# A new issue order for a fused block-sparse attention and SwiGLU kernel: batch 1's V loads before the second half of the output weights, seven more pairs of zero matmuls

## The chip, the cores and the metric

The kernel runs on one core of one Trainium2 chip. TensorE (PE) multiplies matrices and writes to eight banks of PSUM, VectorE (DVE) and ScalarE (ACT) read PSUM and work element by element, GpSimd (POOL) and SyncE (SP) mostly start DMA transfers. Each engine works through its own queue in program order and waits where an instruction needs something that is not there. The metric is the device time of one execution in microseconds, the median of several runs.

## The reference, cut to what matters

```
# attention: B, H, S, D = 4, 8, 768, 64; blocks of 32
scores = scale * np.matmul(q, k.transpose(0, 1, 3, 2))
mask = (|blk_i - blk_j| <= 1) | first or last block in i or j | 3 sampled key blocks per query block
attn = exp(where(mask, scores, -1e9) - max);  attn = attn / (sum(attn) + 1e-9)
attn_out = np.matmul(attn, v)
x = attn_out.transpose(0, 2, 1, 3).reshape(3072, 512)
# feed-forward: d_model 512, d_ff 1536
xn = x / sqrt(mean(x * x) + 1e-6) * rms_g
g = xn @ w_gate;  silu = g * (1 / (1 + exp(-g)))
out = (silu * (xn @ w_val)) @ w_out          # float32, 3072 x 512
```

Inputs and output are float32; the kernel computes its products in bf16.

## The kernel before

The 3072 rows are cut into 12 chunks of 256 queries (`ch` or `u`, 0 to 11), three for each of the 4 batches. The work is cut into some 1,500 named tasks, each with a function that emits its instructions on one engine. For a chunk and a pair of heads `pr` (0 to 3):

- `s<n>` (L648): scores of two key blocks of 128 for a pair of heads, with n = 12 ch + 3 pr + j2, into two PSUM banks; 4 matmuls over 64 rows of the array, two of which run side by side. Chunk 0 adds its mask by matmuls (L653), the others by a multiplication.
- `x<ch>_<pr>_<j2>_<e>` (L661): the exp on ScalarE, one for each bank. `m<ch>_<pr>_<j2>` (L668): the mask product on VectorE.
- `av<ch>_<pr>` (L678): 24 matmuls of probabilities with V (and a column of ones for the sums). `on` (L690, L692): division by the sums on VectorE.
- `sq`, `rs`, `sc` (L703 or L706, L711, L717): RMS norm, the power on GpSimd. `xd` (L741): transposes of x by DMA from SP; chunks 0 and 1 use TensorE (`xt`) and a copy (`xc`).
- `g<u>_<f>a`, `g<u>_<f>` (L835): two times 16 matmuls of gate and value, side by side over 64 rows each; then `th` on ScalarE (L842), `uu` and `h` on VectorE (L846, L853); f is 0 to 5.
- `y<u>_<t>_<part>` (L868): the product with `w_out` in six parts of two matmuls; parts 0 to 2 read the first half of `w_out` (`wo0_`), parts 3 to 5 the second (`wo1_`). `yo` (L890) copies to SBUF and stores from SP.

Loads: batch 0 comes in by small transfers at the start. For batches 1 to 3, K, Q and V (`l<b>_1_*`, `l<b>_0_*`, `l<b>_2_*`, two halves each, L275) go one after the other from GpSimd's queue into one float32 buffer, `stage`: Q cannot start before K's casts have read it (`c<b>_1_*`), nor V before Q's casts (`c<b>_0_*`), nor the next batch's K before V's casts (`va<b>_*`). All casts are L269 and go to ScalarE or VectorE. `dt<b>_*` (L519) then transposes K and Q by DMA from SP. GpSimd also loads the gate and value weights (`wg0_` to `wv2_`, L452) and `wo0_`, `wo1_` (L458). `w<i>` (L321) is a pair of matmuls on zeros that nobody reads; 14 more of them stand at the very start.

The order in which all this is emitted, and so the order in each engine's queue, is written out in the string `ORDER`. A word is a task, `*ENGINE` picks the engine, and the digits after the colon are the buffers that it takes (PSUM banks 0 to 7 first). `ORDER` came out of a planner, whose costs still stand in the calls of `plan.add`, but the class in the file only reads names, engines, functions, dependencies and pools:

```
def add(self, name, engines, fn, deps=(), acq=(), **_):
    self.tasks[name] = (list(engines), fn, [d.lstrip(">") for d in deps],
                        [p for p in acq if p in self.slots])
```

`run` goes through `ORDER` word by word. It asserts that all tasks named in `deps` come earlier and calls the function.

The words of the order before around the second half of `w_out`:

```
... m2_3_2 l1_2_0 wo1_ one1
l1_2_4 s38:47 s39:15 ... va1_0*DVE va1_1*DVE va1_2*DVE va1_3*DVE s41:47 g1_3a:15
... y0_0_0:4 y0_0_1 s44:72 s45:03 y0_0_2 y0_0_3 y0_0_4 y0_0_5 av3_0:6
```

Of the kernel before, what the change touches and what calls it, by code (L numbers as in the profile page):

```python
# [15 lines left out]
sta0 bm q48 rr cast1_0*DVE tsq0 cast0_0*ACT k45 kind0 t0_1_0:0 t0_0_0:1 kr0:2 bs tsq1 e0_1_0*ACT kc0*ACT  # L16
e0_0_0*ACT cast1_1*ACT kind1 w0:3 mq0:4 kr1:5 mq1:6 mq2:7 t0_1_2:0 mqc0*DVE kc1*ACT mqc1*ACT mqc2*ACT
e0_1_2*ACT cast1_2 cast1_3 cast0_1 s0:32 t1_1_0:1 t1_0_0:4 s1:56 s2:70 x0_0_0_0:0 x0_0_0_1 e1_1_0*DVE
e1_0_0*DVE x0_0_1_0 x0_0_1_1 t2_1_0:3 t2_0_0:2 s3:14 s4:56 k67 V0 V4 gB one0 qrest wg0_ wv0_ wg1_ wv1_ wg2_
wv2_ e2_0_0*DVE e2_1_0*DVE x0_0_2_0 x0_0_2_1 x0_1_0_0:1 x0_1_0_1 x0_1_1_0 x0_1_1_1 s5:27 mt1_2:0 mt2_1:3  # L20
t3_1_0:1 t3_0_0:4 w1:5 s6:65 x0_1_2_0 x0_1_2_1 mk2_1*DVE e3_0_0*DVE mk1_2*DVE va0_0*DVE e3_1_0*DVE x0_2_0_0:2
x0_2_0_1 s7:34 mt1_1:2 s8:07 mt0_2:6 s9:51 mk1_1*DVE x0_2_1_0 mk0_2*DVE x0_2_1_1 x0_2_2_0 x0_2_2_1 x0_3_0_0:3
x0_3_0_1 va0_2*DVE av0_0:3 s10:24 s11:60 av0_2:7 t0_0_2:5 mt2_0:1 va0_1*DVE on0_0 on0_2 e0_0_2*DVE va0_3*DVE
mk2_0*DVE x0_3_1_0 x0_3_1_1 x0_3_2_0 x0_3_2_1 sta1_1 t1_0_2:3 mt1_0:2 s12:47 av0_3:6 s13:50 e1_0_2*ACT
x1_0_0_0:4 x1_0_0_1 x1_0_1_0 mk1_0*DVE m1_0_0 on0_3 x1_0_1_1 s14:31 av0_1:4 s15:27 s16:50 t2_0_2:6 x1_0_2_0
x1_0_2_1 on0_1 sq0_0*DVE sq0_1*DVE x1_1_0_0:0 e2_0_2*DVE x1_1_0_1 x1_1_1_0 x1_1_1_1 l1_1_0 l1_1_4 wo0_ rs0
t3_0_2:3 s17:41 w2:2 w3:2 w4:7 w5:2 s18:76 s19:25 mt0_1:0 x1_1_2_0 x1_1_2_1 mk0_1*ACT x1_2_0_0:2 x1_2_0_1
x1_2_1_0 m1_0_1 sc0_0:0 sc0_1:1 e3_0_2*DVE w6:4 w7:4 xt0_0:10 xt0_1:4 s20:07 s21:36 x1_2_1_1 x1_2_2_0 x1_2_2_1
x1_3_0_0:3 xc0_0*DVE xc0_1*DVE m1_1_1 m1_1_2 m1_0_2 m1_2_1 m1_1_0 qk0 raw0 rawq1 xc0 w8:1 w9:2 g0_0a:12 g0_0
s22:45 s23:07 x1_3_0_1 th0_0:0 x1_3_1_0 x1_3_1_1 x1_3_2_0 x1_3_2_1 uu0_0:0 m1_2_2 h0_0:0 m1_3_0 m1_2_0  # L30
g0_1a:36 g0_1 s24:41 g0_2a:50 s25:72 g0_2 th0_1:1 x2_0_0_0:1 x2_0_0_1 x2_0_1_0 x2_0_1_1 th0_2:2 uu0_1:1 h0_1
m1_3_2 uu0_2:2 av1_0:4 s26:17 mt2_2:3 av1_2:2 s27:65 on1_0 m1_3_1 c1_1_0*DVE mk2_2*ACT x2_0_2_0 x2_0_2_1
x2_1_0_0:4 x2_1_0_1 c1_1_1*DVE c1_1_2*DVE c1_1_3*DVE c1_1_4*DVE c1_1_5*ACT h0_2 on1_2 g0_3a:31 s28:47 g0_3
av1_3:6 av1_1:5 w10:0 w11:0 s29:20 sta1_0 th0_3:0 x2_1_1_0 x2_1_1_1 x2_1_2_0 x2_1_2_1 on1_3 uu0_3:0 on1_1 h0_3
m2_0_2 m2_1_1 m2_1_2 sq1_0*ACT sq1_1*ACT l1_0_0 l1_0_4 rs1 s30:46 w12:7 g0_4a:37 g0_4 s31:25 s32:01 th0_4:1
x2_2_0_0:2 x2_2_0_1 x2_2_1_0 x2_2_1_1 x2_2_2_0 x2_2_2_1 uu0_4:1 sc1_0:2 sc1_1:3 h0_4 m2_0_1 m2_2_1 m2_2_0
m2_0_0 m2_2_2 c1_0_0*DVE c1_0_1*DVE c1_0_2*DVE c1_0_3*DVE w13:4 s33:43 w14:6 xt1_0:61 w15:2 xt1_1:5 s34:20
g0_5a:71 g0_5 xc1_0*ACT xc1_1*ACT x2_3_0_0:3 th0_5:2 x2_3_0_1 x2_3_1_0 x2_3_1_1 c1_0_4*ACT c1_0_5*ACT uu0_5:2
m2_3_1 h0_5 qk1 dt1_1_0 dt1_1_3 dt1_0_0 xc1 sta1_2 g1_0a:65 g1_0 g1_1a:43 g1_1 g1_2a:20 g1_2 s35:71 th1_0:0
th1_1:1 x2_3_2_0 x2_3_2_1 th1_2:2 uu1_0:0 uu1_1:1 m2_1_0 h1_0:1 h1_1 uu1_2:2 av2_2:6 mt0_0:4 s36:71 w16:5  # L40
s37:53 av2_0:2 mk0_0*ACT x3_0_0_0:0 x3_0_0_1 x3_0_1_0 x3_0_1_1 m2_3_0 h1_2 on2_0 on2_2 m2_3_2 l1_2_0 wo1_ one1
l1_2_4 s38:47 s39:15 s40:03 av2_1:2 av2_3:6 x3_0_2_0 x3_0_2_1 x3_1_0_0:2 x3_1_0_1 x3_1_1_0 x3_1_1_1 m3_0_1
on2_1 m3_1_0 on2_3 m3_0_2 m3_1_1 m3_0_0 va1_0*DVE va1_1*DVE va1_2*DVE va1_3*DVE s41:47 g1_3a:15 s42:20 s43:36
g1_3 x3_1_2_0 x3_1_2_1 x3_2_0_0:1 x3_2_0_1 x3_2_1_0 x3_2_1_1 th1_3:0 sq2_0 sq2_1 dt1_0_2 dt1_0_4 raw1 rawq2
sta2_1 rs2 l2_1_0 l2_1_4 y0_0_0:4 y0_0_1 s44:72 s45:03 y0_0_2 y0_0_3 y0_0_4 y0_0_5 av3_0:6 x3_2_2_0 x3_2_2_1
yo0_0:0 x3_3_0_0:4 x3_3_0_1 uu1_3:0 m3_1_2 h1_3 sc2_0:0 on3_0 m3_2_0 m3_2_2 m3_2_1 sc2_1:1 s46:17 s47:24
av3_1:5 s48:03 x3_3_1_0 x3_3_1_1 x3_3_2_0 x3_3_2_1 x4_0_0_0:3 x4_0_0_1 g1_4a:61 g1_4 s49:72 av3_2:4 s50:03
x4_0_1_0 th1_4:1 x4_0_1_1 x4_0_2_0 on3_1 m3_3_2 uu1_4:1 m3_3_1 on3_2 h1_4 m3_3_0 x4_0_2_1 g1_5a:57 g1_5 s51:26
s52:03 y0_1_0:4 y0_1_1 y0_1_2 av3_3:1 y0_1_3 th1_5:2 x4_1_0_0:0 x4_1_0_1 x4_1_1_0 c2_1_0*DVE c2_1_1*ACT
x4_1_1_1 c2_1_2*ACT uu1_5:2 on3_3 sq3_0 sq3_1 c2_1_3*DVE h1_5 c2_1_4*DVE c2_1_5*DVE m4_0_2 m4_0_1 xd2_0:2  # L50
xd2_1 qkfree0 xc2 qk2 dt2_1_0 dt2_1_3 sta2_0 l2_0_0 l2_0_4 rs3 y0_1_4 y0_1_5 s53:26 s54:05 g2_0a:31 g2_0
x4_1_2_0 x4_1_2_1 yo0_1:1 th2_0:0 x4_2_0_0:2 x4_2_0_1 uu2_0:0 h2_0:0 g2_1a:72 g2_1 s55:64 g2_2a:03 s56:51 g2_2
th2_1:1 x4_2_1_0 x4_2_1_1 x4_2_2_0 th2_2:2 x4_2_2_1 uu2_1:1 sc3_0:2 h2_1 sc3_1:3 m4_1_2 uu2_2:2 m4_0_0 h2_2
m4_1_1 m4_1_0 m4_2_0 m4_2_1 s57:67 y1_0_0:4 y1_0_1 y1_0_2 y1_0_3 y1_0_4 y1_0_5 s58:52 s59:10 x4_3_0_0:1
x4_3_0_1 yo1_0:2 x4_3_1_0 x4_3_1_1 x4_3_2_0 x4_3_2_1 g2_3a:67 g2_3 s60:43 g2_4a:52 s61:10 g2_4 th2_3:0
x5_0_0_0:4 x5_0_0_1 uu2_3:0 m4_2_2 m4_3_0 m4_3_1 x5_0_1_0 x5_0_1_1 th2_4:1 s62:46 av4_0:3 av4_2:1 av4_1:0
uu2_4:1 on4_0 on4_2 on4_1 m4_3_2 h2_3 h2_4 x5_0_2_0 c2_0_0*ACT x5_0_2_1 s63:45 g2_5a:36 g2_5 s64:10 av4_3:7
y1_1_0:2 y1_1_1 y1_1_2 y1_1_3 x5_1_0_0:3 c2_0_1*ACT c2_0_2*ACT c2_0_3*ACT th2_5:2 x5_1_0_1 on4_3 uu2_5:2
x5_1_1_0 h2_5 m5_0_0 c2_0_4*DVE c2_0_5*DVE x5_1_1_1 sq4_0 sq4_1 xd3_0:3 xd3_1 xc3 dt2_0_0 sta2_2 y1_1_4 y1_1_5
s65:45 g3_0a:71 s66:03 rs4 l2_2_0 l2_2_4 x5_1_2_0 x5_1_2_1 yo1_1:3 x5_2_0_0:2 x5_2_0_1 g3_0 s67:64 g3_1a:52  # L60
g3_1 s68:03 x5_2_1_0 x5_2_1_1 th3_0:0 th3_1:1 x5_2_2_0 x5_2_2_1 g3_2a:64 g3_2 s69:03 th3_2:2 x5_3_0_0:0
x5_3_0_1 va2_0*ACT m5_1_1 sc4_0:0 m5_1_0 uu3_0:0 uu3_1:1 h3_0:1 h3_1 m5_2_2 uu3_2:2 m5_0_2 g3_3a:75 g3_3
s70:12 y2_0_0:0 y2_0_1 y2_0_2 y2_0_3 y2_0_4 y2_0_5 s71:36 x5_3_1_0 th3_3:0 va2_1*ACT x5_3_1_1 va2_2*ACT
yo2_0:0 sc4_1:1 h3_2 m5_0_1 m5_3_1 uu3_3:0 m5_1_2 h3_3 x5_3_2_0 g3_4a:14 g3_4 s72:20 s73:73 y2_1_0:5 y2_1_1
y2_1_2 y2_1_3 x5_3_2_1 th3_4:1 x6_0_0_0:1 x6_0_0_1 uu3_4:1 h3_4 x6_0_1_0 x6_0_1_1 va2_3*ACT m5_2_1 m5_3_0
m5_2_0 m5_3_2 qkfree1 xd4_0:0 xd4_1 xc4 dt2_0_2 dt2_0_4 raw2 rawq3 sta3_1 y2_1_4 s74:62 s75:10 s76:74 av5_0:3
y2_1_5 x6_0_2_0 x6_0_2_1 yo2_1:1 x6_1_0_0:4 x6_1_0_1 x6_1_1_0 x6_1_1_1 av5_2:6 av5_3:2 av5_1:5 s77:10 on5_0
on5_2 m6_0_2 on5_3 on5_1 x6_1_2_0 x6_1_2_1 sq5_0 sq5_1 g3_5a:36 s78:72 g3_5 g4_0a:45 s79:10 g4_0 rs5 l3_1_0
l3_1_4 x6_2_0_0:2 x6_2_0_1 th3_5:2 x6_2_1_0 x6_2_1_1 th4_0:0 m6_1_2 m6_2_0 uu3_5:2 sc5_0:2 uu4_0:0 h4_0:0 h3_5
g4_1a:72 g4_1 g4_2a:13 g4_2 s80:04 th4_1:1 th4_2:2 x6_2_2_0 y3_0_0:5 y3_0_1 y3_0_2 y3_0_3 y3_0_4 y3_0_5 s81:60  # L70
x6_2_2_1 yo3_0:2 x6_3_0_0:0 x6_3_0_1 m6_2_1 uu4_1:1 uu4_2:0 h4_1 m6_2_2 sc5_1:3 h4_2 c3_1_0*DVE m6_1_1
c3_1_1*ACT g4_3a:74 g4_3 s82:12 s83:56 g4_4a:30 g4_4 th4_3:0 x6_3_1_0 m6_3_0 uu4_3:2 m6_1_0 c3_1_2*DVE h4_3
x6_3_1_1 x6_3_2_0 x6_3_2_1 g4_5a:17 g4_5 s84:25 s85:64 th4_4:1 c3_1_3*ACT uu4_4:1 m6_3_2 m6_0_1 c3_1_4*ACT
th4_5:2 x7_0_0_0:3 c3_1_5*ACT x7_0_0_1 x7_0_1_0 x7_0_1_1 uu4_5:0 h4_4 h4_5 m6_3_1 m6_0_0 xd5_0:1 xd5_1 xc5
sta3_0 y3_1_0:3 y3_1_1 y3_1_2 y3_1_3 y3_1_4 y3_1_5 s86:21 s87:50 s88:67 av6_2:4 yo3_1:3 x7_0_2_0 x7_0_2_1
# [88 lines left out]
def kernel(  # L164
# [20 lines left out]
    NP = H // 2  # L185
# [787 lines left out]
```

## Time and profile before

| | |
|---|---|
| time, median of 7 runs | 301.98 us (300.18 to 304.11) |
| the profiled execution | 301.98 us, of which 300.2 us are the span shown |
| granted TensorE clock, mean | 0.994 |
| busy: PE, DVE, ACT, POOL | 96%, 81%, 77%, 12% |
| zero matmuls (L321) | 48, 9.0 us busy |
| HBM read, written | 28.57 MB, 6.29 MB |

The times come from the hardware profiler. A line of waits names the waiting engine and line, the releaser, the sum in us, the number of times and the longest. A line of the timeline gives start and length in us, the engine, the line, the operation, output and input, and the count; in brackets stands the idle time before it and what ended it. Matmuls are pipelined and their ends are modelled, so the distance between two starts says more of TensorE's pace than the busy time.

### The profile page before, as it was taken

What the parts mean: (1) busy time and instruction counts of PE and PEld (TensorE: products, weight loads), DVE (VectorE), ACT (ScalarE), POOL (GpSimd) and SP (SyncE); (2) the same over time, 40 slices, a digit from 0 to 9 for tenths busy, and PEclk for the clock granted to TensorE, in tenths of its full rate; (3) what the DMA queues carried; (4) which work ended last, traced back from release to release, by engine and by line L of the source; (5) the groups of instructions that cost most, each with busy time, mean ns of one, the idle gap of its engine ahead of it and who ended that gap; (6) DMA issues with size and microseconds to landing.
All of it is one profiled execution on the core that took longest, in us unless ns stands there. A gap on an engine that the chain in (4) does not pass through costs nothing.

```text
span 300.2 us, 10723 instructions
## 1 busy us (share of the span) xinstructions
PE 288.1 (96%) x4557; PEld 219.6 (73%) x4579; DVE 243.7 (81%) x501; ACT 232.2 (77%) x469; POOL 35.1 (12%) x56
## 2 busy tenths in 40 slices
PE   8999998994999999999999999999999999999995
PEld 4776987863876876786687678787778778678862
DVE  7579999994889979879988788999759889845840
ACT  7899989896698999987968899998397776242421
POOL 9412021303020030020100021001000000000000
PEclk9999999999899999999999999999999999999999
DMA  8999988894969745668543694612503104224003
GB/s 185 308 204 207 294 137 253 141 225 105 263 75 248 151 83 196 125 163 194 116 186 53 111 239 150 86 40 69 108 2 93 53 2 72 37 38 142 2 9 133
DMA packets 56692, 39.76 MB, mean 132 GB/s; under 512 B 42244, under 2 KB 50052, under 8 KB 56644
## 3 DMA queue, kind: packets, MB, share of 16 engines
q1 hardware_dynamic: 45268, 17.11, 30.3%
q0 software_dynamic: 10688, 21.50, 28.4%
q8 instruction: 36, 0.59, 0.8%
q10 hardware_dynamic: 688, 0.46, 0.5%
q14 instruction: 12, 0.10, 0.1%
HBM read 28.57 MB, written 6.29 MB: 116 GB/s over the span
## 4 chain that ended last, share of the span: by engine, by line
PE 83%; DVE 6%; DMA 5%; ACT 3%; issue 2%; POOL 1%; ACTq 0%
PE f L835 38%; PE f L868 20%; PE f L678 10%; PE f L648 10%; DMA stage<-in_v_dram 5%; ACT pt L661 2%; DVE pt L668 2%; PE f L321 2%; PE f L483 1%; PE f L653 1%; DVE X L692 1%; DVE hp L853 1%; DVE uu L846 1%; PE f L732 1%; DVE va L269 0%
## 5 line engine op out<-in xcount | busy, mean ns | idle before, releaser
L661 ACT ACTIVATE pt<-f 128x512 bf16<-128x512 f32 x288 | 153.5, 645 | 12.8 <-PE f L648 11.5
L835 PE MATMUL f<-xn,wgv 64*128 64x256 bf16 x2304 | 137.7, 270 | 0.3 <-issue 0.3
L835 PEld LDWEIGHTS <-wgv 64*128 64x128 bf16 x2304 | 115.3, 95 | 13.1 <-issue 1.5
L668 DVE TENSOR_TENSOR pt<-pt,Mk 128x1024 bf16<-128x1024 bf16 x132 | 86.4, 685 | 4.1 <-ACT pt L661 4.0
L868 PE MATMUL f<-wo,hp 128*128 128x512 bf16 (+1 forms) x278 | 65.6, 371 | 2.8 <-DMA wo<-in_moe_w_out_dram 1.6
L842 ACT ACTIVATE th<-f 128x512 bf16<-128x512 f32 x72 | 44.1, 619 | 24.7 <-PE f L835 21.7
L846 DVE SCALAR_TENSOR_TENSOR uu<-th,f 128x512 bf16<-128x512 bf16 x72 | 48.6, 683 | 13.8 <-ACT th L842 12.9
L648 PE MATMUL f<-qkT 64*128 64x256 bf16 x576 | 53.3, 273 | 2.1 <-DVE uu L846 1.7
L853 DVE TENSOR_TENSOR hp<-uu,f 128x512 bf16<-128x512 bf16 x72 | 48.3, 683 | 2.2
L868 PEld LDWEIGHTS <-hp 128*128 128x128 bf16 x300 | 27.1, 98 | 31.4 <-issue 5.4
L678 PEld LDWEIGHTS <-pt 128*128 128x128 bf16 x1152 | 38.4, 97 | 8.1 <-issue 4.3
L678 PE MATMUL f<-va,pt 128*128 128x65 bf16 x1152 | 41.0, 194 | 0.9 <-DVE hp L853 0.6
L648 PEld LDWEIGHTS <-qkT 64*128 64x128 bf16 x576 | 26.4, 95 | 14.1 <-issue 10.4
L890 ACT ACTIVATE yo<-f 128x512 f32<-128x512 f32 (+1 forms) x24 | 14.1, 594 | 18.0 <-PE f L868 17.5
L711 POOL TENSOR_TENSOR rs<-ms,nhalf 128x2 f32<-128x2 f32 x12 | 9.1, 755 | 152.1 <-ACT junk L703 132.9
L717 DVE SCALAR_TENSOR_TENSOR x<-X,rs,gB 128x512 bf16<-128x512 f32 (+1 forms) x48 | 22.1, 513 | 3.4 <-POOL rs L711 3.4
L692 DVE TENSOR_TENSOR X<-f,rz 128x256 f32<-128x256 f32 x48 | 20.4, 425 | 1.7
L703 ACT ACTIVATE junk<-X 128x513 bf16<-128x513 f32 x22 | 14.1, 670 | 7.2 <-DVE X L692 7.2
L690 DVE RECIPROCAL rz<-f 128x4 f32<-128x4 f32 x48 | 8.5, 177 | 9.4 <-PE f L678 8.3
L321 PE MATMUL f<-idle 128*128 128x256 bf16 x48 | 9.0, 321 | 2.1 <-DVE idle L296 1.1
L275 POOL DMA_DIRECT2D stage<-in_q_dram x6 | 4.5, 760 | 42.0 <-ACT th L842 15.4
L269 DVE CAST va<-stage 128x768 bf16<-128x768 f32 x10 | 5.3, 552 | 4.4 <-DMA stage<-in_v_dram 4.4
(80 smaller groups left out, 114.7 us busy)
## 6 DMA issues: line engine op xcount, KB each, us to landing
stage<-in_v_dram POOLq DMA_DIRECT2D x8, 768.0 KB, 7.8
out_dram<-yo SPq DMA_DIRECT2D x23, 256.0 KB, 2.2
stage<-in_k_dram POOLq DMA_DIRECT2D x6, 768.0 KB, 7.0
stage<-in_q_dram POOLq DMA_DIRECT2D x6, 768.0 KB, 6.7
wgv<-in_moe_w_gate_dram POOLq DMA_DIRECT2D x3, 512.0 KB, 17.9
wgv<-in_moe_w_val_dram POOLq DMA_DIRECT2D x3, 512.0 KB, 19.8
wo<-in_moe_w_out_dram POOLq DMA_DIRECT2D x2, 768.0 KB, 16.3
xn<-x SPq DMA_TRANSPOSE x40, 3.3
```

The costliest lines, as they stand in the source:

```text
L321: nc.tensor.matmul(out=warm[:, 0:256], lhsT=idle[:, 0:P], rhs=idle, start=True, stop=True)
L648: nc.tensor.matmul(out=s_, lhsT=x[rows, 1, 2 * j2 + jj, pr, :], rhs=x[rows, 0, 2 * ic:2 * ic + 2, pr, :], start=True, stop=not PEM(ch, pr))
L661: nc.scalar.activation(out=pts[ch, pr][:, j2, e], in_=st[t][e], func=AF.Exp, scale=SCALE)
L668: nc.vector.tensor_tensor(out=pv, in0=pv, in1=m.unsqueeze(1).to_broadcast([P, 2, 2 * CQ]), op=ALU.mult)
L678: nc.tensor.matmul(out=o_[:, qt, e, 0:D + 1], lhsT=pt[:, jt // 2, e, jt % 2 * CQ + qt * P:jt % 2 * CQ + (qt + 1) * P], rhs=va[(ch // NIC) ...
L692: nc.vector.tensor_tensor(out=x1s[ch][:, :, 2 * pr * D:(2 * pr + 2) * D].rearrange("p t (h d) -> p t h d", h=2), in0=o4[:, :, :, 0:D], in1 ...
L717: nc.vector.scalar_tensor_tensor(out=x2[:, lo:lo + n], in0=x1s[ch][:, qt, 0:n], scalar=mss[ch][:, qt:qt + 1], in1=gB[:, 0:n], op0=ALU.mult ...
L835: nc.tensor.matmul(out=gst[u, fp, name][:, half * CQ:(half + 1) * CQ], lhsT=wgv[rows, dpart(i, c), f * P:(f + 1) * P], rhs=xns[u][rows, c, :],
L842: nc.scalar.activation(out=ths[u, fp], in_=gst[u, fp, "gp"], func=AF.Tanh, scale=0.5)
L846: nc.vector.scalar_tensor_tensor(out=uus[u, fp], in0=ths.pop((u, fp)), scalar=1.0, in1=gst.pop((u, fp, "gp")), op0=ALU.add, op1=ALU.mult)
L853: nc.vector.tensor_tensor(out=hps[u][:, 2 * fp:2 * fp + 2, :].rearrange("p f t -> p (f t)"), in0=uus.pop((u, fp)), in1=gst.pop((u, fp, "vp ...
L868: nc.tensor.matmul(out=yst[u, t, half][:, 0:n], lhsT=hps[u][:, f, t * P:(t + 1) * P], rhs=wo[:, f, cols], start=(f == 0), stop=(f == NF - 1))
```

## The change

`ORDER` is replaced as a whole. The tasks are the same, but for seven new pairs of zero matmuls. The costs in the `plan.add` calls change too. The change is announced as "issue order and buffers from a model with other DMA transpose durations; second half of the down projection loads ahead of batch 1's V; more zero matmuls". What the new order holds at the places that the prediction speaks of:

```
-    PM1 = 0
+    PMASK = 4
     def PEM(ch, pr):
-        return ch == 0 or ch == 1 and pr < PM1
-    FILL = 17
+        return ch * NP + pr < PMASK
+    FILL = 24
...
-    swdge("V4", ..., 2.4, [">V0"], -9, issue=0.75, extra=2.1)
+    swdge("V4", ..., 2.4, [">V0"], -9, issue=0.75, extra=2.8)
-    swdge("qrest", ..., 2.5, [">gB"], -9, extra=2.1)
+    swdge("qrest", ..., 2.5, [">gB"], -9, extra=3.0)
-    swdge(f"l{b}_{i}_{lo}", ..., (3.6, 2.5, 2.5)[i],
+    swdge(f"l{b}_{i}_{lo}", ..., 2.6,
-    plan.add(f"dt{b}_{i}_{c0}", ..., dma=0.7 * (c1 - c0), prio=1)
+    plan.add(f"dt{b}_{i}_{c0}", ..., dma=1.2 * (c1 - c0), prio=1)
-    plan.add(f"xd{ch}_{qt}", ..., dma=1.1, extra=1.6 + XSLACK,
+    plan.add(f"xd{ch}_{qt}", ..., dma=1.6, extra=1.6 + XSLACK,
...
 in ORDER (extracts):
-... xc1_0*ACT xc1_1*ACT x2_3_0_0:3 th0_5:2 x2_3_0_1 x2_3_1_0 x2_3_1_1 c1_0_4*ACT c1_0_5*ACT
+... x2_3_0_0:2 x2_3_0_1 th0_5:2 xc1_0*ACT c1_0_0*ACT c1_0_1*ACT c1_0_2*ACT c1_0_3*ACT x2_3_1_0 x2_3_1_1 c1_0_4*ACT c1_0_5*ACT xc1_1*DVE
-... l1_2_0 wo1_ one1 l1_2_4 s38:47 s39:15 s40:03 ...
+... l1_2_0 l1_2_4 wo1_ one1 w20:0 s38:02 av2_2:7 s39:56 w21:1 s40:31 ...
-... g1_3 ... y0_0_0:4 y0_0_1 s44:72 s45:03 y0_0_2 y0_0_3 y0_0_4 y0_0_5 av3_0:6 s46:17 s47:24 av3_1:5 s48:03 g1_4a:61
+... g1_3 ... s44:02 y0_0_0:5 y0_0_1 av3_0:7 y0_0_2 s45:14 y0_0_3 y0_0_4 y0_0_5 s46:70 s47:21 w22:4 w23:4 g1_4a:54
-... dt2_1_0 dt2_1_3 sta2_0 l2_0_0 l2_0_4 rs3 ... xd3_0:3 xd3_1 xc3 dt2_0_0
+... dt2_1_0 rs3 l2_0_0 l2_0_4 ... xd3_0:3 sta2_2 xd3_1 dt2_1_3 xc3 dt2_0_0
-... yo11_1:0 yo11_2:1 yo11_0:2 yo10_0:3 yo10_1:0
+... yo11_2:0 yo10_0:1 yo11_0:2 yo11_1:3 yo10_1:0
```

## The prediction, made before the changed kernel ran

> **What bounds the kernel now.** I read the page first (busy shares), then a table of stages, then the waits of TensorE, then the chain of waits where the stages fall short.
>
> ```profile
> PE 288.1 (96%) x4557; PEld 219.6 (73%) x4579; DVE 243.7 (81%) x501; ACT 232.2 (77%) x469; POOL 35.1 (12%) x56
> ...
> 25.00:45.00 20.00, 19.61 (x338) 16.34 (x339) 19.76 (x45) 18.62 (x38) 2.27 (x3) 1.00 1.05 214
> 45.00:66.00 21.00, 19.90 (x351) 16.08 (x348) 20.86 (x43) 19.54 (x41) 3.32 (x5) 1.00 0.94 201
> 66.00:72.00 6.00, 4.05 (x43) 2.16 (x43) 1.63 (x4) 4.71 (x13) 0.72 (x1) 1.00 0.62 145
> 72.00:82.00 10.00, 8.06 (x132) 6.63 (x133) 9.17 (x21) 6.28 (x13) 1.54 (x2) 0.83 0.98 218
> 82.00:265.00 183.00, 181.50 (x2913) 137.66 (x2928) 158.10 (x309) 150.25 (x306) 14.36 (x19) 1.00 0.49 110
> ```
>
> Columns: stretch, length, then busy time of PE, PEld, DVE, ACT and POOL, the granted clock, DMA share, GB/s. Three regimes. From 25 to 66 us VectorE (19.8 of 20, 20.9 of 21) and ScalarE are full and TensorE follows them. From 82 us TensorE is full (181.5 of 183), so whatever it has fallen behind by then stays in the span. Between them, 66 to 82 us, nobody is full: this is the time to be had.
>
> ```profile
> PE f L648 <- DVE uu L846: 1.7, 1, 1.7
> PE f L868 <- DMA wo<-in_moe_w_out_dram: 1.6, 1, 1.6
> ...
> 55.06 0.79 POOL stage L275
> 55.85 0.84 POOL wo L458
> 56.70 0.09 POOL va L462
> 56.79 14.87 DMA stage<-in_v_dram
> 71.66 0.02 issue
> 71.68 1.03 DVE va L269 x2
> 72.71 0.61 DVE uu L846
> ```
>
> The first two lines are TensorE's longest waits; the rest is the chain of waits in its order of time. GpSimd issues half of batch 1's V, then the second half of `w_out` (`wo1_`), then the other half of V, which lands 14.87 us later. VectorE's queue stands at `va1_2` meanwhile:
>
> ```profile
> 66.29 1.02 DVE L269 CAST va<-stage 128x768 bf16<-128x768 f32 x2
> 71.68 1.03 DVE L269 CAST va<-stage 128x768 bf16<-128x768 f32 x2 [4.37 <-DMA stage<-in_v_dram]
> ...
> 69.50 1.46 PE L868 MATMUL f<-wo,hp 128*128 128x512 bf16 x6 [1.58 <-DMA wo<-in_moe_w_out_dram]
> 70.80 0.89 PE L678 MATMUL f<-va,pt 128*128 128x65 bf16 x24
> 73.36 0.61 PE L648 MATMUL f<-qkT 64*128 64x256 bf16 x8 [1.67 <-DVE uu L846]
> 74.56 1.46 PE L678 MATMUL f<-va,pt 128*128 128x65 bf16 x24 [0.59 <-DVE hp L853]
> ...
> 67.80:71.20 3.40, 1.82 (x21) 0.98 (x20) 0.00 (x0) 2.11 (x7) 0.72 (x1) 1.00 0.48 115
> 71.20:74.60 3.40, 1.14 (x27) 0.92 (x23) 2.92 (x6) 2.20 (x5) 1.54 (x2) 1.00 0.28 88
> 74.60:78.00 3.40, 3.40 (x44) 2.77 (x45) 3.37 (x8) 2.32 (x5) 0.00 (x0) 0.50 0.97 314
> ```
>
> VectorE idle for 4.37 us makes TensorE wait 1.67 + 0.59 = 2.26 us for banks and masks. And after the thin stretch 71.2 to 74.6 the clock is granted at 0.50 for 3.4 us: the same 24 matmuls of an `av` take 1.46 us instead of 0.89. That costs another 1.7 us (half of 3.4).
>
> **The change part by part.**
>
> The planner's numbers (`dma`, `extra`, the loads' 2.6) are swallowed by `**_` in `Plan.add`: they emit nothing. `PMASK = 4` gives the old set (chunk 0). What remains is `ORDER` and `FILL`.
>
> *`wo1_`.* The words of the change say that it loads ahead of batch 1's V. The order says otherwise: before `l1_2_0 wo1_ one1 l1_2_4`, now `l1_2_0 l1_2_4 wo1_ one1`, and the instructions on GpSimd follow it. So V goes first.
> - V: the next batch's two halves, issued together, took 6.3 us (median) from issue to landing. The first now starts after `c1_0_5`. All six `c1_0` casts are on ScalarE, behind `xc1_0`. I walked the new order by the durations of these rows: `xc1_0` ends at 50.5, six casts of 0.5 and two exps of 0.48 give 54.5 (54.77 before). So issue at 54.7 and 55.5, landing near 62 and 65 with the batch's transposes in the way. VectorE wants the second half at 66.6: the 4.37 us are gone, TensorE's 2.26 with them, and the half clock with the thin stretch: **-2.26 - 1.7**.
> - `wo1_` is now last of the three. The same bytes go through the same 16 engines, so I let the last landing stay at 71.66 less the 0.4 of the earlier issue: 71.2. It was 69.46 (55.85 + 13.6). `y0_0_3` waits for it: **+1.74**. Ahead of it now stands `av3_0` (24 matmuls, 0.73 from start to start) that stood behind: **-0.73**. Queued behind `y0_0_3` on TensorE are `s46`, `s47`, `g1_4`, so the exps of ScalarE wait for it too. Bounds for the landing: 65.6 (V's 6.3 us from its issue at 55.5, then 768 packets at the 200 a us that the gate and value weights reached in the trace between 20 and 30 us) and 75.2 (issue at 56.3 + 18.9, what the first half took in a full queue). The value taken is nearest to the row of the same three loads.
>
> *`FILL` 17 to 24.* 14 more zero matmuls (L321). A pair takes 0.214 us at full clock, 1.5 us in all. Seven of the 24 pairs stand at 40 to 43 us in the walk, where TensorE waits for exps anyhow: hidden. `w22 w23` behind `y0_0` are half covered by the copy of `y0_0` that frees a bank: **+0.2**. With the cover gone everywhere: +1.5.
>
> Here the Trainium skill speaks ("TensorE: Matmul & The Clock Gate", Part 1): the clock halves after an idle window of about 3.4 us. By that rule a wait of 2.5 us (68.7 to 71.2) at `y0_0_3` leaves the clock alone. The row says less: 71.2 to 74.6 held 1.14 us of matmuls and the clock still fell, while 1.82 of 3.4 kept it. So 2.3 us of idleness can do it, and a wait of 2.5 us does it when it falls into one window. By the rule the sum stands; by the row it loses 1.7 us in some runs. The extra zero matmuls stand behind that wait, not in it. I take no fall, since the wait must lie nearly whole in one window, and keep the other as a rival.
>
> *Engines.* Up to the end of chunk 3's scores ScalarE gives away `mqc2`, `e1_0_2`, `c1_1_5`, `xc1_1`, two squares and two mask copies (4.5 us) and takes `e2_0_0`, two mask copies and `c1_0_0` to `c1_0_3` (3.5 us): -1.0. VectorE's sum up to `va1_3` grows by 0.1. Walking banks and queues, chunk 3's first exp stands at 59.15 (59.09 before): **0**. ScalarE waits at `th0_2` and `th0_3` in place of the old 1.31 us before `x2_3_2_0`. If the walk is off by a slip per stage, 0 is -1 to +1.5.
>
> *After 82 us.* A step between a 64-row matmul (L835, L648) and a 128-row one (L868, L678) costs something: by the starts in the timeline from 85 to 265 us, from scores to `y` 0.22 where 0.055 is usual, from `y` to scores 0.31 against 0.216, so some 0.13 each. The new order has 41 such steps after `s51` and had 47: **-0.8**. Other moves cost nothing: `rs3` is now ahead of batch 2's Q on GpSimd; `one0` waits behind `wv1_` until about 10 us, wanted at 14.5; on SP `dt2_1_3` goes past `xd3` and two stores, its reader is chunk 6, 60 us later. GpSimd now has `rs2` ahead of batch 2's K, about 69.3, four us earlier than 73.0; its cast is wanted by ScalarE at 78.4 and it lands at 76 to 78.
>
> *Tail.* `yo11_0` and `yo11_1` move behind `yo10_0`; their 1.0 us fits into the 2.2 of `y10_1`, but two more stores are in flight with the last: **+0.2** (0 to 1.0).
>
> **Sum:** -2.26 - 1.7 + 1.74 - 0.73 + 0.2 - 0.8 + 0.2 = -3.35. The profiled execution took 301.98 us (span 300.2 and 1.8 around it), which is also the median of the runs shown: 298.6 us.
>
> **Rivals.**
> - *A, as summed* (0.40): 298.6, own range 297.2 to 300.0.
> - *B, the clock falls at the new wait* (0.22): 1.7 more, 300.3. For: the row above; the wait is longer than 1.58. Against: it must fall into one window.
> - *C, slower: the loads start late and `wo1_` is last* (0.25). All `c1_0` casts are in ScalarE's queue, behind th and exp that wait for TensorE. If `wo1_` lands at 75.2, `y0_0_3` waits 4.0 us more, 302.6, and a wait of 6.5 us surely halves the clock: 304.3. It decides from a landing at 72.9 on (1.7 + 1.7 eat the gain). For: the first half took 18.9 us. Against: five weight loads and K's two halves were then still ahead of it; now V's two halves are.
> - *D, more comes back* (0.13): `wo1_` at 69 and the walk 0.5 us early: 297.0 to 295.8.
>
> That the planner's numbers do nothing by themselves is read from the code, not a rival.
>
> **How the numbers follow.** About 1% (3.0 us) is what a measurement of this kernel tells from no change; the line is 298.96. A lies below it for two thirds (0.26), D nearly whole (0.12), B hardly (0.02): faster 0.40. C is over 305.0 only where a late start adds to the clock, half of it: slower 0.13. The rest, 0.47, is within 1%. The range 295.8 to 305.0 takes D's end and C with its clock.
>
> **What would show it.** Right: no idle time of VectorE before `va`; one wait of TensorE for `wo` of about 2.5 us near 68.7; no waits for `uu` or `hp` there; `g1_5` done near 79 us (82.05 now); 82 to 265 us of before about 0.8 shorter. B: a granted clock of 0.50 near 72 to 76. C: a wait for `wo` above 4 us, `c1_0_5` ending after 56. Wrong altogether: VectorE or ScalarE idle for more than 3 us between 25 and 66.

## The result, and the profile after

The changed kernel took **299.15 us** (median of 13 runs, 297.63 to 305.88) beside 301.96 us for the kernel before (34 runs): a ratio of 0.9905, 95% interval 0.9879 to 0.993. That is 2.9 us or 0.95% less (2.1 to 3.7 us); 298.6 was predicted. Two of the 13 executions (302.23 and 305.88 us) ran slow and are left out of the ratio. The profiled execution took 298.77 us with a span of 297.0 (300.2 before).

The table of stages of the kernel after, in the columns of the one shown of before:

```profile
25.00:45.00 20.00, 19.29 (x305) 14.29 (x303) 19.54 (x42) 18.18 (x37) 2.27 (x3) 1.00 1.12 212
45.00:66.00 21.00, 20.47 (x370) 16.58 (x368) 20.76 (x43) 18.16 (x36) 3.66 (x5) 1.00 0.94 229
66.00:72.00 6.00, 5.95 (x80) 3.65 (x78) 5.97 (x13) 6.00 (x15) 1.46 (x2) 1.00 0.45 74
72.00:82.00 10.00, 9.76 (x172) 7.41 (x170) 9.76 (x22) 7.89 (x17) 0.77 (x2) 1.00 1.14 240
82.00:265.00 183.00, 181.32 (x2931) 139.52 (x2950) 157.98 (x305) 150.69 (x309) 14.09 (x19) 1.00 0.47 110
67.80:71.20 3.40, 3.35 (x40) 1.82 (x40) 3.37 (x8) 3.40 (x10) 0.66 (x1) 1.00 0.11 16
71.20:74.60 3.40, 3.29 (x47) 2.21 (x47) 3.37 (x7) 3.40 (x8) 1.57 (x3) 1.00 0.54 130
74.60:78.00 3.40, 3.32 (x78) 2.70 (x74) 3.30 (x7) 3.26 (x8) 0.00 (x0) 1.00 1.00 359
```

The hole is filled: from 66 to 72 us TensorE is busy for 5.95 us (4.05 before) and VectorE for 5.97 (1.63), and the stretch from 74.6 to 78 runs at a clock of 1.00 (0.50). But DMA in the window 67.8 to 71.2 is down to a share of 0.11, where 0.48 stood: the loads were over by then, earlier than predicted. ScalarE's 18.16 of 21 us in the second row (19.54 before) has two reasons: it has less work there, as the prediction counts, and it waited more ahead of the hole (its waits stand further below).

The timeline of the kernel after around the same place (start and length in us, then engine, line, operation):

```profile
56.74 1.53 POOL L275 DMA_DIRECT2D stage<-in_v_dram  x2 [9.40 <-ACT qb L269]
58.27 0.85 POOL L458 DMA_DIRECT2D wo<-in_moe_w_out_dram  x1
...
65.24 0.55 DVE L269 CAST va<-stage 128x768 bf16<-128x768 f32 x1
67.46 1.49 DVE L269 CAST va<-stage 128x768 bf16<-128x768 f32 x3
...
67.79 1.04 PE L868 MATMUL f<-wo,hp 128*128 128x512 bf16 x3
68.67 0.89 PE L678 MATMUL f<-va,pt 128*128 128x65 bf16 x24
69.40 0.59 PE L868 MATMUL f<-wo,hp 128*128 128x512 bf16 x2
69.92 0.39 PE L648 MATMUL f<-qkT 64*128 64x256 bf16 x4
70.25 1.47 PE L868 MATMUL f<-wo,hp 128*128 128x512 bf16 x6
71.65 0.64 PE L648 MATMUL f<-qkT 64*128 64x256 bf16 x8
72.40 0.60 PE L321 MATMUL f<-idle 128*128 128x256 bf16 x4
...
79.14 0.60 PE L648 MATMUL f<-qkT 64*128 64x256 bf16 x8
...
80.45 0.62 ACT L269 CAST kb<-stage 128x512 bf16<-128x512 f32 x1 [1.97 <-DMA stage<-in_k_dram]
```

Nothing stands in brackets behind the casts of V or behind the products with `wo`: neither waits. `s51`, the scores right behind `g1_5`, starts at 79.14, where it started at 82.05. The line of ScalarE at 80.45 is new: the first cast of batch 2's K waits 1.97 us for its load. The waits of the kernel after:

```profile
ACT kb L269 <- DMA stage<-in_k_dram: 2.0, 1, 2.0
...
PE f L868 <- DVE uu L846: 0.5, 1, 0.5
...
PE f L835 <- ACT Mk L565: 0.3, 1, 0.3
```

Both long waits of TensorE (1.7 and 1.6 us) are gone and the 2.5 us predicted in their place did not come. By the starts of the same tasks in both traces:

| stretch | before, us | after, us | difference | predicted |
|---|---|---|---|---|
| start to `s24` | 34.01 | 34.48 | +0.47 | 0 |
| `s24` to chunk 3's first exp | 25.08 | 26.29 | +1.21 | 0 |
| that exp to `s51` | 22.96 | 18.37 | -4.59 | -2.75 |
| `s51` to `s60` | 15.28 | 16.26 | +0.98 | -0.8 for |
| `s60` to `y10_1_5` | 198.72 | 197.42 | -1.30 | both |
| the rest | 4.15 | 4.18 | +0.03 | +0.2 |

They add up to the 3.2 us of the spans. The total was hit with two steps that were 1.7 and 1.8 us off, in opposite directions.

### The profile page after: what moved, and what is told of

Read it like the earlier page. It is cut to its first block, busy times and chain, and to the rows that moved or that the text cites. A ratio compares the mean times of both kernels' runs of the same rounds, so it can differ in the third digit from the quotient of the medians.

```text
span 297.0 us, 10760 instructions
## 1 busy us (share of the span) xinstructions
PE 288.8 (97%) x4570; PEld 218.7 (74%) x4593; DVE 246.1 (83%) x503; ACT 230.7 (78%) x467; POOL 35.2 (12%) x56
## 4 chain that ended last, share of the span: by engine, by line
PE 69%; ACT 4%; DMA 3%; DVE 2%; issue 1%; POOL 0%; POOLq 0%; DVEq 0%; ACTq 0%
PE f L835 34%; PE f L868 19%; PE f L678 8%; PE f L648 7%; DMA stage<-in_k_dram 3%; ACT pt L661 2%; ACT junk L703 1%; DVE hp L853 1%; DVE uu L846 1%; DVE pt L668 0%; ACT th L842 0%; DVE x L717 0%; POOL stage L275 0%; POOL rs L711 0%; PE f L321 0%
## 5 line engine op out<-in xcount | busy, mean ns | idle before, releaser
L678 PE MATMUL f<-va,pt 128*128 128x65 bf16 x1152 | 40.3, 193 | 0.2
L648 PEld LDWEIGHTS <-qkT 64*128 64x128 bf16 x576 | 26.9, 94 | 12.4 <-issue 8.0
L703 ACT ACTIVATE junk<-X 128x513 bf16<-128x513 f32 x20 | 13.0, 661 | 8.9 <-DVE X L692 8.9
L321 PE MATMUL f<-idle 128*128 128x256 bf16 x62 | 11.1, 310 | 1.5 <-DVE idle L296 1.1
L275 POOL DMA_DIRECT2D stage<-in_v_dram x8 | 6.2, 777 | 40.0 <-ACT qb L269 26.1
L269 ACT CAST qb<-stage 128x512 bf16<-128x512 f32 x17 | 9.6, 637 | 0.0
## 6 DMA issues: line engine op xcount, KB each, us to landing
wgv<-in_moe_w_val_dram POOLq DMA_DIRECT2D x3, 512.0 KB, 20.8
```

What stands on the lines that cost most here:

```text
L648: nc.tensor.matmul(out=s_, lhsT=x[rows, 1, 2 * j2 + jj, pr, :], rhs=x[rows, 0, 2 * ic:2 * ic + 2, pr, :], start=True, stop=not PEM(ch, pr))
L678: nc.tensor.matmul(out=o_[:, qt, e, 0:D + 1], lhsT=pt[:, jt // 2, e, jt % 2 * CQ + qt * P:jt % 2 * CQ + (qt + 1) * P], rhs=va[(ch // NIC) ...
L703: nc.scalar.activation(out=junk, in_=x, func=AF.Square, scale=float(DM) ** -0.5, accum_out=ms)
```

## The experiments

"Before" below is the kernel before on the same chip: 301.94 us for the first four, 302.19 for the next four, 302.12 for the last three. Times are medians of 6 to 22 executions; differences in us come from the ratios.

### Is it V's place, and does `wo1_` pay for it?

e1: the kernel before with only the loads reordered.

```
-... l1_2_0 wo1_ one1 l1_2_4 s38:47 ...
+... l1_2_0 l1_2_4 wo1_ one1 s38:47 ...
```

> The kernel before with one change: wo1_ and one1 stand behind both halves of batch 1's V. Theory 1 (the gain is V's place: VectorE's 4.4 us wait, the 2.3 us of TensorE behind it and the half clock) expects nearly the whole gain: 2.5 to 3.5 us below before, no DMA wait of VectorE at va, a wait for wo of 1 to 3 us at y0_0_3. Rival R1 (the new order as a whole, of which V's place is a part among many) expects at most 1.2 us.

Measured: 299.91 us, ratio 0.9942 (0.9921 to 0.9962), so 1.75 us less. V's second half landed at 65.91 and nobody waited for it, but `wo1_`, issued at 57.30, landed only at 71.45, after 14.1 us. Among its waits:

```profile
PE f L868 <- DMA wo<-in_moe_w_out_dram: 2.9, 1, 2.9
```

From `s24` to `s51` this trace is 2.69 us shorter than before. The terms of the prediction for this edit alone (-2.26, -1.7, and the wait grown from 1.6 to 2.9) give -2.66. So in the trace V's place is worth what was said, and in *this* order `wo1_` does pay, as predicted. The time is another matter: 1.75 us (1.1 to 2.4) lies between the two expectations, below the 2.5 to 3.5 of theory 1 and above the rival's 1.2. In the changed kernel `wo1_` does not pay. What differs is the order around the loads, not the loads.

e2: the reverse, the changed kernel with `wo1_` between the halves again.

```
-... l1_2_0 l1_2_4 wo1_ one1 w20:0 ...
+... l1_2_0 wo1_ one1 l1_2_4 w20:0 ...
```

> The changed kernel with wo1_ back between the two halves of V. Theory 1 expects the gain gone: 0 to 1 us above before, since the new order reaches this place about 1.9 us later than the old; VectorE's wait at va_2 is back with 2 to 4 us, and the clock falls to 0.50 once. R1 expects 1.5 us or more still below before.

Measured: 300.2 us, ratio 0.9934 (0.99 to 0.9968); against the changed kernel's 0.9905 this is about 0.9 us slower, and the intervals overlap. The trace is clearer: `wo1_` landed at 66.84, V's second half at 70.03, and in the timeline of this kernel VectorE stands before `va1_2`:

```profile
70.06 1.03 DVE L269 CAST va<-stage 128x768 bf16<-128x768 f32 x2 [2.15 <-DMA stage<-in_v_dram]
```

TensorE's wait behind it is 1.3 us, `s24` to `s51` 2.2 us longer than in the changed kernel. By `s60` 0.8 of it has come back: the wait of ScalarE for K is then 0.44 us instead of 1.97.

Theory 1's expectation failed here. VectorE's wait is back as expected, but the clock stayed at 1.00, and the time is 2.0 us below before where 0 to 1 above was expected; it is the rival R1 that expected 1.5 or more below. With the old order of loads V is only 2.15 us late, not 4.37, and two thirds of the gain remain. In the traces (2.0 us between the spans) `s24` to `s51` is 1.2 us shorter than before and the part from `s60` on 1.3 us, with 0.5 lost elsewhere. So V's place is a part of what the new order gains, not nearly the whole.

### The half clock, and the zero matmuls

e4: the kernel before with seven pairs of zero matmuls inside the thin stretch, V left as late as it was.

```
-... sc2_1:1 s46:17 s47:24 av3_1:5 ...
+... sc2_1:1 w<i>:7 (seven of them) s46:17 s47:24 av3_1:5 ...
```

> The kernel before with seven pairs of zero matmuls more, all between av3_0 and s46, where TensorE waits 1.67 us for VectorE. They take 1.5 us at full clock, so they fit into the wait. If the half clock after it was a cost of its own, it goes and the time falls by 1 to 1.7 us; the waits for uu and hp stay. If the clock had nothing to do with the idle stretch, the time stays within 0.4 us of before.

Measured: 300.9 us, ratio 0.9963 (0.9944 to 0.9981), 1.1 us less (0.6 to 1.7). The three windows of this kernel:

```profile
67.80:71.20 3.40, 1.50 (x8) 0.62 (x7) 0.00 (x0) 2.10 (x6) 0.72 (x1) 1.00 0.82 190
71.20:74.60 3.40, 2.99 (x48) 2.42 (x45) 2.15 (x4) 1.63 (x4) 0.82 (x2) 1.00 0.24 87
74.60:78.00 3.40, 2.61 (x56) 2.31 (x54) 3.37 (x9) 3.06 (x6) 0.72 (x1) 1.00 0.79 241
```

With 2.99 us of matmuls, most of them on zeros, in the stretch that held 1.14, the clock stays at 1.00. So the thin stretch did cause the half clock, and that cost 1.1 us by the times (V landed 0.8 us later in this profile, which may have eaten a part). The term -1.7 is at the upper end of the interval.

e3: the changed kernel without `w17` to `w23`.

```
-FILL = 24          ... w20:0 s38:02 ... w22:4 w23:4 g1_4a:54
+FILL = 17          ... s38:02 ... g1_4a:54
```

> The changed kernel without its last seven pairs of zero matmuls (w17 to w23). Theory 1 with the pairs hidden expects no more than 0.3 us to either side of the changed kernel. Rival R2 (the pairs stand on TensorE's path and cost their 1.5 us) expects 1.0 to 1.5 us below the changed kernel. Rival R3 (they are what keeps the clock) expects the clock to fall at 68 to 76 us and 1 to 2 us more than the changed kernel.

Measured: 298.95 us, ratio 0.9913 (0.9881 to 0.9946), no different from the changed kernel. No cost and no gain of the seven pairs can be seen (`s24` to `s51` is 0.1 us shorter in the trace); the predicted +0.2 is below what the times tell apart.

### Why `wo1_` was not late

The changed kernel issues V 1.7 us later than before, yet the last of the three loads lands at 69.79 instead of 71.66. One theory is the place in the DMA queues: `dt1_0_4`, the last transposes of batch 1's Q, is issued at 56.48, just ahead of V's 56.74; before it came at 56.03, behind V's 55.06. The other is that the order of the loads alone sets it, and an earlier V is better.

e6: the changed kernel with V's issue brought forward, by two casts ahead of two exps on ScalarE.

```
-... c1_0_3*ACT x2_3_1_0 x2_3_1_1 c1_0_4*ACT c1_0_5*ACT ...
+... c1_0_3*ACT c1_0_4*ACT c1_0_5*ACT x2_3_1_0 x2_3_1_1 ...
```

> The changed kernel with c1_0_4 and c1_0_5 ahead of two exps on ScalarE, so that V and wo1_ are issued about 1 us earlier (55.7) and the transposes dt1_0_2, dt1_0_4 have less of a start. Theory 2 (the loads are slow when the batch's transposes are still in the DMA queues beside them) expects wo1_ to land no earlier than 69.8, more likely at 70.5 to 71.5, in spite of the earlier issue, and dt1_0_2 to land at 60 or later. The rival (a fixed 11.5 us from issue to landing) expects it at 68.8. The time: within 0.5 us of the changed kernel by either, up to 1 us more by theory 2.

Measured: 300.74 us, ratio 0.994 (0.9913 to 0.9967), some 1.0 us slower than the changed kernel (the intervals overlap), with a wait of 2.0 us for `wo`. Not all of it is the loads' doing: the casts push two exps back as well, and chunk 3's first scores (`s36`) start 26.9 us after `s24` instead of 25.9. V was issued at 55.76, and `dt1_0_4` at 56.12 now stands behind it. For the tile `wo`, the time from issue to landing in the changed kernel, then in e6:

```profile
DMA to landing us min/median/max: 11.5/11.5/11.5
```

```profile
DMA to landing us min/median/max: 16.3/16.3/16.3
```

`wo1_` was issued 1.0 us earlier and landed 3.8 us later (73.58 against 69.79). The DMA queues between 62 and 66 us (q0: loads from GpSimd; q1: from SP, here transposes), of the changed kernel:

```profile
DMA packets 567, 1.17 MB, mean 293 GB/s; under 512 B 34, under 2 KB 382, under 8 KB 567
...
q0 software_dynamic: 565, 1.17, 110.2%
q1 hardware_dynamic: 2, 0.00, 0.0%
```

and of e6:

```profile
DMA packets 313, 0.41 MB, mean 103 GB/s; under 512 B 225, under 2 KB 241, under 8 KB 312
...
q0 software_dynamic: 90, 0.34, 96.0%
q1 hardware_dynamic: 222, 0.06, 13.1%
```

In both the load queue fills the 16 engines (110% and 96%), but beside 222 transpose packets of 256 B it moved 0.34 MB where it moved 1.17 without them. On the mean a load packet held an engine for 4 us x 16 x 0.96 / 90 = 0.68 us. That mean hides two kinds. By the single packets in the trace of e6, those of 4,608 B took 0.19 us at the median, no more than in the changed kernel with no transposes beside them (80 a us between 63 and 64 us, 0.20 us each). But 11 load packets that began between 62.4 and 64.2 us took 2.9 to 4.0 us; in the changed kernel none of the three loads' packets took over 1 us. So in this window e6 lost its time to packets that stood still, and not to turns taken by small ones. Why they stood still is not shown.

e10: e6 with `dt1_0_4` taken out of the way, issued behind chunk 0's first store.

```
-... dt1_0_2 dt1_0_4 raw1 rawq2 sta2_1 ... yo0_0:0 m3_1_2 ...
+... dt1_0_2 sta2_1 ... yo0_0:0 dt1_0_4 raw1 rawq2 m3_1_2 ...
```

> Kernel e6_after_v_earlier (V issued at 55.8, wo1_ landing at 73.6) with one more move: dt1_0_4, the last transposes of batch 1's Q, is issued from SP behind the first store of chunk 0 (near 73) instead of at 56.1; chunk 5 reads it only near 95. Theory 1 (the transposes that lie between and behind V in the DMA queues delay wo1_): with none in the queues wo1_ lands 66 to 68.5, the wait for wo is 0, V's second half lands by 67, time 298.5 to 299.7 (e6 300.74 less its 2.0 us wait, less or more a slip). Theory 2 (it is V's own early issue, or wo1_'s bytes, that makes it late): wo1_ lands at 71.5 or later, the wait stays above 1 us, 300.2 to 301.2.

Measured: 300.66 us, ratio 0.9956 (0.9926 to 0.9987). The landing did what the queue theory says: V's second half at 63.13, `wo1_` at 66.76, and for the tile `wo`

```profile
DMA to landing us min/median/max: 10.5/10.5/10.5
```

with no wait for it. But the time did not move: it lies above the 298.5 to 299.7 of theory 1, in the range of theory 2, though the landing rules theory 2 out. The transposes now issued at 73.33 lie ahead of `x`'s for chunk 2, behind K's two loads, and those of `x` landed at 83.06 to 85.97. TensorE's longest wait, for `wo` in e6, is another here:

```profile
PE f L835 <- DMA xn<-x: 1.7, 1, 1.7
```

2.0 us were taken out and 1.7 came back 15 us later (`s24` to `s51` is 2.15 us shorter than in e6, `s51` to `s60` 2.0 longer): at both places the transposes delayed what was in flight beside them.

The three loads, from the first V issue to the last landing, in all kernels of this case:

| `dt1_0_4` issued | kernels | us | transpose packets of 256 B meanwhile | load packets over 1 us |
|---|---|---|---|---|
| ahead of V by 0.26 to 0.27 | after, e2, e3, e5, e8, e9 | 13.1, 13.4, 13.2, 13.0, 13.1, 12.7 | 1,137 to 1,448 | 0, in e9 1 |
| behind the first half of V | before, e1, e4, e6, e7 | 16.6, 15.7, 17.2, 17.8, 15.2 | 2,160 to 2,637 | 2, 17, 17, 23, 18 |
| not among them (near 73) | e10, e11 | 12.0, 11.8 | 1,138, 144 | 0 |

No kernel stands in the wrong row. Issued ahead, the transposes cost the loads about 1.2 us; issued a fraction of a microsecond behind, 3.3 to 6. The packets that stand still for over 1 us belong almost wholly to the second row.

### Can the kernel before be mended the same way?

e7: e1, and `av3_0` ahead of the second half of the product with `w_out`.

```
-... s45:03 y0_0_2 y0_0_3 y0_0_4 y0_0_5 av3_0:6
+... s45:03 av3_0:6 y0_0_2 y0_0_3 y0_0_4 y0_0_5
```

> The kernel before with wo1_ behind V (as in the first of these runs, which was 1.75 us below before and waited 2.9 us for wo at y0_0_3) and with av3_0 ahead of y0_0_2. By the sum of the prediction av3_0's 0.73 us come out of the wait: 2.2 us are left, and the time is 0.7 us lower than in that run. Rival: av3_0 itself waits there for VectorE's m3_0 or va1_0, and nothing is gained.

Measured: 299.72 us, ratio 0.9936 (0.9902 to 0.997), as e1 within the interval; the 0.7 us expected do not show in the times (`s24` to `s51` is 0.6 us shorter). The wait for `wo` is 1.7 instead of 2.9 us, so `av3_0` does fill it, but the loads, still in the second row of the table, stay late. The profiled execution had a half clock between 20.8 and 27.6 us of its own (see the last section), so its absolute times are not used.

e8: e7, and the last two casts of Q behind two `th` on ScalarE. That delays V, and puts `dt1_0_4` ahead of it.

```
-... x2_3_1_1 c1_0_4*ACT c1_0_5*ACT ... sta1_2 ... th1_0:0 th1_1:1 x2_3_2_0
+... x2_3_1_1 ... th1_0:0 th1_1:1 c1_0_4*ACT c1_0_5*ACT sta1_2 x2_3_2_0
```

> The kernel of the run before this one, with c1_0_4 and c1_0_5 behind th1_0 and th1_1 on ScalarE, where it stood idle for 1.3 us: V and wo1_ are issued about 2 us later (57.0), and the transposes are ahead of them. Theory 2 expects dt1_0_2 to land near 58 and wo1_ at 69.5 to 70.5, a wait for wo below 1.2 us, and 0.7 to 1.3 us less time than the run before this one. The rival with a fixed time from issue to landing (14.1 us) expects wo1_ at 73 and 1.5 us more.

Measured: **297.92 us**, ratio 0.9869 (0.9843 to 0.9895), the best of all. `dt1_0_4` at 55.85 is ahead of V at 56.12, and `wo1_` takes 11.6 us instead of 13.7. From the first issue to the last landing the three loads take 13.1 us instead of 15.2. But the wait for `wo` was expected to fall below 1.2 us and is 1.6 (e7: 1.7). Counted from `s24`, V is issued 2.3 us later than in e7, and `wo1_` lands after 36.5 us against 36.3, so the faster loads only made up for their later start. From `s24` to `y10_1_4` the traces of e7, e8 and the changed kernel take 258.2, 258.8 and 257.9 us. Two or three edits on the kernel before thus do about as well as the new order; the lead of e8 over e7 (2.0 us by the times) is not explained by its loads. The profiles differ ahead of `s24` (32.74 against 38.11, see the last section), and e8 has only six executions.

e11: e8 with `dt1_0_4` issued behind the first store, the edit of e10.

> Kernel e8_before_late_casts with dt1_0_4 issued behind the first store of chunk 0 in place of 55.85. Theory 1 (transposes in the queues delay the loads): wo1_, issued near 57.6, lands 66 to 67.5 in place of 69.25, the wait of 1.6 us for wo goes, and what VectorE and ScalarE can follow comes back: 296.4 to 297.4 us. Theory 2 (with the transposes ahead of V the queue is as fast as it gets): wo1_ lands at 68.5 to 69.5, time as e8, 297.6 to 298.4. Against both: the transposes at 73 push x's transposes of chunk 2 back by 1 to 2 us; if those are late, TensorE waits near 90 and it is slower than e8 by up to 1 us.

Measured: 300.18 us, ratio 0.9941 (0.991 to 0.9972), about 2 us slower than e8 (up to 1 us was expected). `wo1_` took 10.25 us and its wait fell to 0.3, but `xn` was late by 1.6 us again. The third guess, that `x`'s transposes are pushed back, holds: `s24` to `s51` is 1.7 us shorter than in e8, `s51` to `s60` 1.8 longer. From `s24` to `y10_1_4` that leaves 258.5 us against 258.8, so the 2 us between the medians are again not explained by the loads.

### Batch 2's K

e5: the changed kernel with K's two loads ahead of `rs2` on GpSimd.

```
-... rs2 l2_1_0 l2_1_4 ...
+... l2_1_0 l2_1_4 rs2 ...
```

> The changed kernel with batch 2's K (l2_1, two loads) ahead of rs2 on GpSimd. In the changed kernel rs2 waits for chunk 2's squares until 70.3, K is issued at 71.2 and lands at 80.2, and ScalarE stands 1.97 us at c2_1_0. Theory K (this wait costs TensorE the 1 us that it lost between 79 and 95) expects issue near 69, landing near 78, ScalarE's wait below 0.5 us, and 0.5 to 1.0 us below the changed kernel. Rival: TensorE has other work then, and the time stays within 0.3 us.

Measured: 298.54 us, ratio 0.988 (0.9834 to 0.9925): not to be told from the changed kernel by time. The timeline of this kernel:

```profile
70.41 1.51 POOL L275 DMA_DIRECT2D stage<-in_k_dram  x2 [9.51 <-DVE va L269]
...
79.89 0.68 ACT L269 CAST kb<-stage 128x512 bf16<-128x512 f32 x1
```

The cast no longer waits, and `s51` to `s60` takes 15.28 us, exactly what it took before, in place of 16.26. So K's late load was the 0.98 us lost there. Of it 0.7 is lost again ahead of `s51` in this trace (`s24` to `s51` takes 45.34 us against 44.67), for a reason that these runs do not show.

e9: the same on e8, where K's second half landed at 76.25, in time.

> Kernel before with wo1_ behind both halves of V, av3_0 ahead of y0_0_2, the last two Q casts behind two th (as e8_before_late_casts), and batch 2's K ahead of rs2 on GpSimd. Theory 'K pays only where it is late': in e8_before_late_casts K's second half landed at 76.25, before ScalarE and VectorE come to its casts, so landing 1 us earlier is worth nothing: 297.5 to 298.3 us, as e8 (297.92). Rival 'every microsecond of K is passed on': 0.8 to 1.4 us faster, 296.5 to 297.1.

Measured: 298.89 us, ratio 0.9897 (0.986 to 0.9933). `s51` to `y10_1_4` is 213.61 us against 213.73 in e8: no gain, as K was not late there. The median is above the expected 297.5 to 298.3, with an interval (297.9 to 300.1) that reaches into it.

## Why the prediction was right or wrong

**The bound, and V's place: right as a mechanism.** VectorE's 4.37 us, TensorE's 2.26 us of waits and the half clock went together. e1 shows that reordering three loads is enough for all three; e4 puts the clock at 0.6 to 1.7 us, 1.7 predicted. But e2 gains 2.0 us with V late again, so the change does not hang on V's place alone. The words of the change ("ahead of batch 1's V") were rightly set aside for what the order says.

**`wo1_` makes TensorE wait, +1.74: wrong, by 3.3 us.** The wait was to grow from 1.58 to over 3 us, less what `av3_0` covers; there was none. Two things took it away. `wo1_` landed at 69.79, 1.4 us ahead of the predicted 71.2, though not ahead of the 69.46 of before. And TensorE came to `y0_0_3` only at 70.25, where 68.7 was predicted, because everything ahead of it had slipped (see "Chunk 3's first exp" below). Each alone would have left a wait of about 1 us.

The failed sentence on the landing is "the same bytes go through the same 16 engines, so I let the last landing stay": the bytes were the same, but what they share the engines with was not. The transposes were "in the way" in the prediction only as a quantity, not as a place in the order. In the trace of before it could have been read, between 62 and 66 us:

```profile
q0 software_dynamic: 601, 0.65, 90.5%
q1 hardware_dynamic: 593, 0.15, 28.8%
```

601 load packets and 593 transpose packets are one for one. The Trainium skill ("DMA: Bandwidth & Descriptors", "Queues, rings and completion order") says that each DMA engine takes turns between its queues, a packet at a time, which fits these counts. The 580 packets of `wo1_` among them took 0.096 us each, as they do alone (0.098), but 145 a us went through where 200 do alone: some 1.1 us lost in these 4. Turns are not the whole loss, though. In e6 the counts are 90 to 222, and the time went into a few packets that stood still for 2.9 to 4.0 us; neither the page nor the runs say why.

**`av3_0` ahead, -0.73: wrong by its premise.** It was to fill the wait for `wo`; with no wait it is only a move. e7 shows that it does fill one where there is one: 1.7 instead of 2.9 us.

**Chunk 3's first exp at 59.15, "0": wrong, +1.7.** It came at 60.77, and `c1_0_5` ended at 56.45, not 54.5. 0.47 us were lost before `s24`. The rest is ScalarE waiting for TensorE; its waits between 34 and 62 us, before:

```profile
ACT pt L661 <- PE f L648: 2.1, 2, 1.3
ACT th L842 <- PE f L835: 0.4, 2, 0.2
ACT Mk L565 <- PE f L558: 0.3, 1, 0.3
```

and after:

```profile
ACT pt L661 <- PE f L648: 2.8, 4, 1.0
ACT th L842 <- PE f L835: 1.9, 3, 0.7
```

4.7 us against 2.8. The walk had two of these waits, at `th0_2` and `th0_3`, and took them to stand in for the old 1.31; it missed those for scores before `x2_0_1_0`, `x2_0_2_0` and `x2_3_0_0`, and at `th1_2` and the first exp itself (0.72 and 1.04 us). Adding up ScalarE's tasks by their durations is not enough where TensorE releases so many of them. The slip went just past the bound of +1.5.

**The two errors belong together.** The later issue of V is what put `dt1_0_4` ahead of it. Sign C ("`c1_0_5` ending after 56") came true, and its consequence did not: the later issue meant a faster load. e6 undoes the delay, and its loads take 17.8 us instead of 13.1. And a slip ahead of a wait is taken out of that wait: the 1.7 us by which everything came later were 1.7 us more for `wo1_` to land.

**B, no:** no half clock near 72 to 76. With no wait there, its step was not put to the test in the changed kernel; e1 does test it. Its wait for `wo` is 2.85 us (68.64 to 71.49), longer than the 2.5 of B, and the clock stayed at 1.00. In the traces the changes of the granted clock stand whole steps of 3.4 us apart (64.8 us, 19 steps, in before; 17.1 us, 5 steps, in e7). Counted in such steps from the first change, e1's wait is cut in two:

```profile
67.00:70.40 3.40, 1.63 (x12) 0.57 (x12) 3.40 (x8) 3.40 (x9) 0.81 (x1) 1.00 1.29 150
70.40:73.80 3.40, 2.31 (x34) 1.54 (x35) 1.39 (x4) 0.84 (x3) 1.85 (x3) 1.00 0.52 114
```

The stretch of before with 1.14 us of matmuls was one whole step. So what B said against itself, that the wait must fall into one window, is what these traces show; a limit in busy time they do not give (the last section has 1.53 and 1.57).

**After `s51`, -0.8: right in kind.** From `s60` on the trace is 1.30 us shorter; ahead of it 0.98 is lost to K's load. The step that failed was K's issue "about 69.3": `rs2` hangs on the same slip of the walk, so K was issued at 71.21 and landed at 80.22, not 76 to 78. e5 shows the price. That the remaining gain comes from fewer switches between 64-row and 128-row matmuls was not tried.

**Zero pairs and tail, +0.2 each: right to be small.** e3 finds nothing for the pairs, the tail shows +0.03.

Put together with the measured terms: -2.26 - 1.58 and -0.6 to -1.7 for the clock make -4.4 to -5.5 for the hole, where the trace has -4.59; +1.68 for the walk; -0.3 after it: -3.2. That 298.6 came so near is luck: -3.3 for the wait at `wo` was met by +1.7 of the walk, +0.73 of `av3_0` and +0.98 of the lost K.

## What to carry to other kernels

When a load is late, read which packets share the engines with it, not only how many bytes are ahead of it: in these kernels small transposes issued just behind a large load stretched the loads by 3.3 to 6 us, and issued just ahead by about 1.2. Moving them away handed the delay to the next transfer (e10, e11), so move them to where nothing in flight is wanted soon. A faster load that starts later by the same amount gains nothing (e8). And a predicted total that comes out right is no proof of its terms: compare the traces stretch by stretch.

## What the runs showed of the hardware that was not expected

With V issued 1 us earlier, the load behind it landed 3.8 us later (e6); on the way 11 load packets of 4,608 B took 2.9 to 4.0 us each, in place of 0.2.

The loads also have a pace of their own: with nothing beside it `wo1_`, in packets of 1,024 B, moved some 200 packets a us, about 205 GB/s, while V in packets of 4,608 B reached about 370 (changed kernel, 63 to 68 us).

When TensorE first reaches full clock changes from one execution to the next: by the start-to-start times of the first scores (0.207 us at half, 0.103 at full clock) and the first grant in the trace, after 3.7 us in the profile of e7, 4.9 in that of e8, 10.1 in that of the changed kernel and 13 in that of e5. In e1, e3 and e4 it then fell back for one step of 3.4 us, though 2.3 to 2.7 us of the step before held matmuls.

In e7 the clock fell back to 0.50 from 20.8 to 27.6 us. TensorE had waited 2.04 us for `qb` (19.5 to 21.5), and the step ahead of the fall held 1.53 us of matmuls:

```profile
17.40:20.80 3.40, 1.53 (x36) 1.11 (x32) 2.16 (x6) 3.05 (x7) 0.00 (x0) 1.00 1.28 204
20.80:24.20 3.40, 2.68 (x25) 1.41 (x26) 1.78 (x4) 0.58 (x1) 0.74 (x1) 0.50 1.26 205
```

In e6 a step with 1.57 us (71.8 to 75.2) was not followed by a fall. Busy time alone therefore does not tell these two apart.

Such differences ahead of `s24` (32.74 in e8, 38.11 in e7) are why stretches are compared here from `s24` on, and why medians of a few executions are read with care.
